# A sliding-window attention and FFN block: attention moved from token-major to channel-major layout

## Chip, cores and metric

The kernel runs on one core of a Trainium2 chip. The metric is the device time of one execution in microseconds (us). A core has five engines that each work through their own instructions in order and wait for each other by semaphores: TensorE (PE; its weight loads are listed apart as PEld), VectorE (DVE), ScalarE (ACT), GpSimd (POOL) and SyncE (SP, which issues most transfers).

## What is computed

With x of 2048 tokens by 640 channels, 32 heads of 20 channels, a window of 8 tokens with dilation 2, and an FFN of width 1536, all in bf16 at the interface:

```python
xn = layernorm(x)
q, k, v = split(xn @ wqkv)                       # 32 heads of 20 channels each
idx = pos[:, None] - 2 * arange(8)[None, :]      # the 8 tokens that a token attends to
logits = einsum("bhsd,bhswd->bhsw", q, k[idx]) * 20 ** -0.5
logits = where(idx >= 0, logits, -1e9)
o = einsum("bhsw,bhswd->bhsd", softmax(logits), v[idx])
out = x + o @ wo + (gelu_tanh(xn @ w1 + b1) @ w2 + b2)
```

## The kernel before

The 2048 tokens are taken in four blocks `n` of 512 tokens (`CH`), each of four pieces `bl` of 128 tokens. Channels are five tiles of 128 (`KT`). All weights are loaded at the start, nearly all by SP, in the order in which the code issues them: four pieces of x, the rest of x (`x_all`), the Q and K weights (`wqk_sb`), V's weights, `b1_rt`, `b2bc`, the two FFN weights, and the output projection `wo2`.

- Layer norm (`ln_units`): DVE takes statistics of all tokens at the start, ACT normalizes one piece, PE transposes it, and ACT copies it to `xnT` (channels on partitions, tokens free).
- Q and K (`qk_units`, L241, L252) come out with channels on partitions, as `qTn` and `kTn`. `kTn` has 14 columns ahead, taken from the block before, so a shift by 2w tokens is a slice.
- V (`v_units`, L267, L270) comes out with tokens on partitions. ACT copies it and writes it to DRAM (`v_tok`). `issue_vwin` (L298) reads it back through POOL's queue, as `vwin`, eight shifted copies of each piece, 1280 KB each.
- Logits (`logit_units`): for a half block of 256 tokens (`pr`) and a window position `w`, DVE multiplies Q by the shifted K (`prod`, L380). Then PE takes each 128x128 part of `prod` as weights and multiplies it by `ind`, 128x32, which sums the channels of each head (L388). The result `lg` has tokens on partitions and (window position, head) in the free dimension.
- Softmax (`softmax_unit`, L342 to L364): maximum, subtraction, `exp` on ACT, sum, reciprocal, `attn`, by half block.
- Weighted sum of V (`av_units`): DVE multiplies `vwin` by `attn` (L415) and adds the upper four window positions to the lower (L421); PE adds the remaining four by matmuls against `ident` and transposes in doing so (L439); ACT copies to `oTn`.
- FFN (`ffn1_units`, L314, L321) and output (`out_units`, L465 to L494): an output piece is one PSUM sum of 12 FFN tiles, 5 attention tiles and x + b2 (`xb2`), in a pair of tiles `ops_lo` (512 columns) and `ops_hi` (128). ACT copies it out.

The order of work is written out by hand: `interleave` puts one or two `fillers` (FFN, next block's layer norm, Q, K, V) ahead of each `prod` step, and `inserts` say after which step the softmax and the weighted sum stand. Four PSUM banks (`psum1`) serve all but the logits and the output.

Of the kernel before, what the change touches and what calls it, by code (L numbers as in the profile page):

```python
# [12 lines left out]
ALU = mybir.AluOpType  # L14
# [6 lines left out]
def kernel(  # L21
# [11 lines left out]
):  # L33
    nc = tc.nc
# [15 lines left out]
    HP = 2 * P  # L50
    NPR = BPC // 2
    WH = W // 2
    SCALE = float(DH) ** -0.5
    EPS = 1e-5
    A3 = 0.044715
    GC = math.sqrt(2.0 / math.pi)
    SQA3 = math.sqrt(A3)
    PADC = PAD + CH
    PSW = 2 * CH

    assert Bb == 1 and D == KT * P and F == FT * P and S == NCH * CH
    assert P == 4 * H and FT % 2 == 0 and BPC % 2 == 0 and NCH == 4
# [7 lines left out]
    dram = ctx.enter_context(tc.tile_pool(name="dram", bufs=1, space=bass.MemoryType.DRAM))  # L70
    psum1 = ctx.enter_context(tc.tile_pool(name="psum1", bufs=4, space=bass.MemoryType.PSUM))
    psumL = ctx.enter_context(tc.tile_pool(name="psumL", bufs=2, space=bass.MemoryType.PSUM))
    psumO = ctx.enter_context(tc.tile_pool(name="psumO", bufs=2, space=bass.MemoryType.PSUM))

    ident = consts.tile([P, P], BF16, name="ident")
    make_identity(nc, ident[:])

    x0p = ctx.enter_context(tc.tile_pool(name="x0p", bufs=1))
    x0 = x0p.tile([P, BPC, D], BF16, name="x0")
    for bl in range(BPC):  # L80
        nc.sync.dma_start(x0[:, bl, :], x_nb[:, bl, :])
    tmp = tc.alloc_tile_pool(name="tmp", bufs=1, side="right")
    x_all = tmp.tile([P, NB, D], BF16, name="x_all")
    for c in range(1, NCH):
        nc.sync.dma_start(x_all[:, c * BPC : (c + 1) * BPC, :], x_nb[:, c * BPC : (c + 1) * BPC, :])
    wqk_sb = wts.tile([P, KT, 2 * D], BF16, name="wqk_sb")
    wqkv_v = A_wqkv.rearrange("(t p) n -> p t n", p=P)
    nc.sync.dma_start(wqk_sb[:, :, 0:D], wqkv_v[:, :, 0:D])
    nc.sync.dma_start(wqk_sb[:, :, D : 2 * D], wqkv_v[:, :, D : 2 * D])
    wv_raw = tmp.tile([P, KT, D], BF16, name="wv_raw")  # L90
    nc.sync.dma_start(wv_raw[:], wqkv_v[:, :, 2 * D : 3 * D])
    b1_rt = tmp.tile([P, P], BF16, name="b1_rt")
    nc.sync.dma_start(b1_rt[0:FT, :], B_b1.rearrange("(t p) -> t p", p=P))
    b2bc = consts.tile([P, D], BF16, name="b2bc")
    b2_bcast = bass.AP(tensor=B_b2.tensor, offset=B_b2.offset, ap=[[0, P], [1, D]])
    nc.sync.dma_start(b2bc[:], b2_bcast)
    w1_sb = wts.tile([P, KT, F], BF16, name="w1_sb")
    nc.sync.dma_start(w1_sb[:], B_w1.rearrange("(t p) n -> p t n", p=P))
# [3 lines left out]
    for t in range(KT):  # L102
        for q in range(4):
            src = bass.AP(
                tensor=A_wo.tensor,
                offset=A_wo.offset + (4 * t + q) * D,
                ap=[[DH * D, H], [1, D]],
            )
            nc.sync.dma_start(wo2[q * H : (q + 1) * H, t, :], src)
    zeros = tmp.tile([P, D], BF16, name="zeros")  # L110
    nc.vector.memset(zeros[:], 0.0)
    v_tok = dram.tile([PAD + S, D], BF16, name="v_tok")
    nc.sync.dma_start(v_tok[0:PAD, :], zeros[0:PAD, :])

    ind_f = tmp.tile([P, KT, H], F32, name="ind_f")
    nc.gpsimd.memset(ind_f[:], 1.0)
    nc.gpsimd.affine_select(
        out=ind_f[:],
        in_=ind_f[:],
        pattern=[[P, KT], [-DH, H]],  # L120
        compare_op=ALU.is_ge,
        fill=0.0,
        base=0,
        channel_multiplier=1,
    )
    nc.gpsimd.affine_select(
        out=ind_f[:],
        in_=ind_f[:],
        pattern=[[-P, KT], [DH, H]],
        compare_op=ALU.is_ge,  # L130
        fill=0.0,
        base=DH - 1,
        channel_multiplier=-1,
    )
    ind = consts.tile([P, KT, H], BF16, name="ind")
    nc.vector.tensor_copy(ind[:], ind_f[:])
    eps_t = consts.tile([P, 1], F32, name="eps_t")
# [5 lines left out]
    mv_all = tmp.tile([P, NB, nc.vector.BN_AGGR_DIM], F32, name="mv_all")
    std_all = tmp.tile([P, NB], F32, name="std_all")
    rstd_all = consts.tile([P, NB], F32, name="rstd_all")
    negmb_all = consts.tile([P, NB], F32, name="negmb_all")
    for sl, src, boff in ((slice(0, BPC), x0, 0), (slice(BPC, NB), x_all, BPC)):
        for b in range(sl.start, sl.stop):
            stats = tmp.tile([P, 2, nc.vector.BN_STATS_DIM], F32, name=f"stats{b}")
            xb_ = src[:, b, :] if src is x_all else src[:, b, :]  # L150
            nc.vector.bn_stats(stats[:, 0, :], xb_[:, 0 : D // 2])
            nc.vector.bn_stats(stats[:, 1, :], xb_[:, D // 2 : D])
            nc.vector.bn_aggr(mv_all[:, b, :], stats[:])
        nc.scalar.activation(std_all[:, sl], mv_all[:, sl, 1], ACT.Sqrt, bias=eps_t[:], scale=1.0)
        nc.vector.reciprocal(rstd_all[:, sl], std_all[:, sl])
        nc.vector.scalar_tensor_tensor(
            out=negmb_all[:, sl],
            in0=mv_all[:, sl, 0],
            scalar=-1.0,
            in1=rstd_all[:, sl],  # L160
            op0=ALU.mult,
            op1=ALU.mult,
        )
    b1_tp = psum1.tile([P, PSW], BF16, tag="acc1", name="b1_tp")
# [3 lines left out]
    for ti in range(KT):  # L168
        nc.vector.tensor_copy(
            out=wv_perm[:, ti, :].rearrange("p (d h) -> p d h", d=DH),  # L170
            in_=wv_raw[:, ti, :].rearrange("p (h d) -> p d h", d=DH),
        )

    tmp.release()

    xtp = ctx.enter_context(tc.tile_pool(name="xtp", bufs=2))
    ktp = ctx.enter_context(tc.tile_pool(name="ktp", bufs=2))
    qtp = ctx.enter_context(tc.tile_pool(name="qtp", bufs=2))
    lnp = ctx.enter_context(tc.tile_pool(name="lnp", bufs=3))
    vsp = ctx.enter_context(tc.tile_pool(name="vsp", bufs=2))  # L180
    prodp = ctx.enter_context(tc.tile_pool(name="prodp", bufs=2))
    smp = ctx.enter_context(tc.tile_pool(name="smp", bufs=2))
    atp = ctx.enter_context(tc.tile_pool(name="atp", bufs=6))
    vwp = ctx.enter_context(tc.tile_pool(name="vwp", bufs=3))
    avp = ctx.enter_context(tc.tile_pool(name="avp", bufs=1))
    otp = ctx.enter_context(tc.tile_pool(name="otp", bufs=1))
# [486 lines left out]
```

## Time and profile before

| | before |
|---|---|
| time, median of 3 runs | 288.19 us (286.31 to 289.06) |
| profiled execution: time | 287.44 us |
| profiled execution: span, first to last instruction | 285.3 us |
| mean granted TensorE clock | 0.976 of full speed |
| busy: PE, DVE, ACT, POOL | 242.8, 169.4, 136.1, 17.9 us |
| HBM read, written | 35.56 MB, 5.26 MB |

The profile is one execution. Busy time of PE includes the tail of each matmul, in which the next one runs already. In its rows, `line engine op out<-in xcount | busy us, mean ns | idle before it <- who ended that idle time`; in a row of the timeline, the first two numbers are the start and the length in us.

### The profile page before, as it was taken

Reading aid. Unit: us, or ns where it says so; the run is one execution under the profiler, and the core shown is the slowest. Engines: PE = TensorE matmul, PEld = TensorE weight load, DVE = VectorE, ACT = ScalarE, POOL = GpSimd, SP = SyncE. Lnnn points to the kernel's source line nnn. Section 1 sums busy time; section 2 is a strip of 40 time slices with the busy share of each in tenths; the row PEclk is TensorE's granted clock in tenths of the full one; section 3 lists DMA queues with packets and bytes.
Section 4 is the critical chain, followed back from the end, with each engine's and each line's share of the span. In section 5 each row is a group of like instructions: output and inputs, shape, how many; then the busy total and the mean of one; then the engine's idle time right before and its main releaser. Section 6 shows DMA issues by size and latency. Waiting matters only on the chain. (4 is left out here: it accounts for less than half of the span.)

```text
span 285.3 us, 5189 instructions
## 1 busy us (share of the span) xinstructions
PE 242.8 (85%) x2177; PEld 140.7 (49%) x2217; DVE 169.4 (59%) x221; ACT 136.1 (48%) x240; POOL 17.9 (6%) x29
## 2 busy tenths in 40 slices
PE   0028996539999999999899999999899999998895
PEld 0023453414455645566565445566555565565552
DVE  5892041817436517449994614799997876618810
ACT  1333559149647977452227884532226753332221
POOL 2000022000100000001111000001101111100000
PEclk9999999559999999999999999999999999999999
DMA  6999339940602010024767000026666287551010
GB/s 200 368 381 355 83 115 317 361 146 4 229 3 75 32 36 0 2 92 160 245 231 258 32 0 3 23 71 233 207 232 210 60 294 239 166 176 38 30 37 25
DMA packets 20507, 41.15 MB, mean 144 GB/s; under 512 B 1782, under 2 KB 15748, under 8 KB 20484
## 3 DMA queue, kind: packets, MB, share of 16 engines
q0 software_dynamic: 4352, 20.97, 21.1%
q1 hardware_dynamic: 11524, 14.61, 16.2%
q10 hardware_dynamic: 4608, 5.24, 5.2%
q8 instruction: 17, 0.28, 0.4%
q14 instruction: 6, 0.05, 0.0%
HBM read 35.56 MB, written 5.26 MB: 143 GB/s over the span
## 5 line engine op out<-in xcount | busy, mean ns | idle before, releaser
L380 DVE TENSOR_TENSOR prod<-qTn,kTn 128x1280 bf16<-128x1280 bf16 x64 | 51.0, 820 | 60.3 <-PE lg L388 43.6
L314 PE MATMUL hps<-xnT,w_sb 128*128 128x512 bf16 x233 | 55.4, 384 | 0.9 <-ACT hTn L321 0.3
L481 PE MATMUL ops_lo<-w_sb,hTn 128*128 128x512 bf16 x177 | 52.2, 380 | 3.2 <-ACT osb L492 3.1
L415 DVE TENSOR_TENSOR avprod<-vwin,attn 128x5120 bf16<-128x5120 bf16 x16 | 45.1, 2820 | 8.4 <-PE oacc_hi L439 8.4
L241 PE MATMUL qkps<-xnT,wqk_sb 128*128 128x512 bf16 x194 | 47.4, 391 | 1.3 <-ACT xnT L212 1.0
L484 PE MATMUL ops_hi<-w_sb,hTn 128*128 128x128 bf16 x192 | 42.2, 220 | 0.8 <-issue 0.2
L314 PEld LDWEIGHTS <-w_sb 128*128 128x128 bf16 x240 | 23.1, 99 | 26.6 <-issue 2.2
L321 ACT ACTIVATE hTn<-hps,b1T 128x512 bf16<-128x512 f32 x48 | 31.2, 688 | 6.5 <-PE hps L314 5.9
L388 PEld LDWEIGHTS <-prod 128*128 128x128 bf16 x640 | 23.0, 97 | 16.3 <-DVE prod L380 9.3
L388 PE MATMUL lg<-ind,prod 128*128 128x32 bf16 x640 | 25.7, 178 | 5.6 <-DVE prod L380 5.4
L241 PEld LDWEIGHTS <-wqk_sb 128*128 128x128 bf16 x200 | 18.9, 100 | 22.6 <-issue 3.9
L481 PEld LDWEIGHTS <-hTn 128*128 128x128 bf16 x192 | 18.7, 98 | 19.5
L492 ACT CAST osb<-ops_lo 128x512 bf16<-128x512 f32 x16 | 9.4, 585 | 39.6 <-PE ops_lo L481 39.5
L446 ACT CAST oT<-oacc_lo 128x512 bf16<-128x512 f32 x16 | 9.3, 584 | 31.4 <-PE oacc_lo L439 31.0
L421 DVE TENSOR_TENSOR avprod<-avprod 128x2560 bf16<-128x2560 bf16 x16 | 23.6, 1475 | 0.2
L298 POOL DMA_DIRECT2D vwin<-v_tok x16 | 14.3, 891 | 144.7 <-DVE avprod L415 139.8
L481 PE MATMUL ops_lo<-wo,oT 128*128 128x512 bf16 x74 | 22.3, 379 | 0.1
L267 PE MATMUL vlo<-wv_perm,xnT 128*128 128x512 bf16 x75 | 22.0, 379 | 0.0
L439 PEld LDWEIGHTS <-avprod 128*128 128x128 bf16 x320 | 18.1, 98 | 6.2 <-DVE avprod L421 5.7
L484 PEld LDWEIGHTS <-hTn 128*128 128x128 bf16 x192 | 18.7, 98 | 4.3 <-issue 4.1
L439 PE MATMUL oacc_lo<-ident,avprod 128*128 128x128 bf16 x256 | 17.0, 219 | 2.2 <-DVE avprod L421 2.0
L484 PE MATMUL ops_hi<-wo,oT 128*128 128x128 bf16 x80 | 17.5, 219 | 0.3
(59 smaller groups left out, 240.1 us busy)
## 6 DMA issues: line engine op xcount, KB each, us to landing
vwin<-v_tok POOLq DMA_DIRECT2D x16, 1280.0 KB, 7.1
w_sb<-in_B_w_dram SPq DMA_DIRECT2D x2, 1920.0 KB, 17.5
v_tok<-v_sb ACTq DMA_DIRECT2D x16, 160.0 KB, 1.8
xb<-in_A_x_dram SPq DMA_DIRECT2D x16, 160.0 KB, 5.3
out_dram<-osb ACTq DMA_DIRECT2D x16, 160.0 KB, 2.4
x_all<-in_A_x_dram SPq DMA_DIRECT2D x3, 640.0 KB, 7.5
xt<-in_A_x_dram SPq DMA_DIRECT2D x12, 160.0 KB, 2.8
wqk_sb<-in_A_wqkv_dram SPq DMA_DIRECT2D x2, 800.0 KB, 10.4
```

Source lines behind the costliest of these rows:

```text
L241: nc.tensor.matmul(ps[:], lhsT=wqk_sb[:, ti, to * P : (to + 1) * P], rhs=xnT[:, ti, :], start=(ti == 0), stop=(ti == KT - 1),)
L267: nc.tensor.matmul(vlo[:], lhsT=lhs, rhs=wv_perm[:, ti, 0:CH], start=(ti == 0), stop=(ti == KT - 1))
L298: nc.gpsimd.dma_start(vwin[:], vsrc)
L314: nc.tensor.matmul(hps[:], lhsT=w1_sb[:, ti, ft * P : (ft + 1) * P], rhs=xnT[:, ti, :], start=(ti == 0), stop=(ti == KT - 1),)
L321: nc.scalar.activation(hTn[:, ft, :], hps[:], ACT.Gelu_apprx_tanh, bias=b1T[:, ft : ft + 1], scale=1.0)
L380: nc.vector.tensor_tensor(out=prod[:], in0=qTn[:, :, pr * HP : (pr + 1) * HP], in1=kTn[:, :, PAD - DIL * w + pr * HP : PAD - DIL * w + (pr ...
L388: nc.tensor.matmul(lg[:, q * HP + w * H : q * HP + (w + 1) * H], lhsT=prod[:, t, q * P : (q + 1) * P], rhs=ind[:, t, :], start=(t == 0), s ...
L415: nc.vector.tensor_tensor(out=avprod[:].rearrange("p w (d h) -> p w d h", d=DH), in0=vwin[:].rearrange("p w (d h) -> p w d h", d=DH), in1= ...
L421: nc.vector.tensor_tensor(out=avprod[:, 0:WH, :], in0=avprod[:, 0:WH, :], in1=avprod[:, WH:W, :], op=ALU.add,)
L439: nc.tensor.matmul(dst, lhsT=avprod[:, j, t * P : (t + 1) * P], rhs=ident[:], start=(j == 0), stop=(j == WH - 1),)
L481: nc.tensor.matmul(ops_lo[:], lhsT=lhs, rhs=rhs[:, 0:CH], start=(k == 0), stop=(k == nk - 1))
L484: nc.tensor.matmul(ops_hi[:, 0 : D - CH], lhsT=lhs, rhs=rhs[:, CH:D], start=(k == 0), stop=(k == nk - 1),)
```

## The change

Attention stays on chip in one layout, channels on partitions and tokens free.

- V is projected like Q and K, to `vT` with 14 columns ahead; `v_tok`, `vwin` and their transfers go. `wqkv_sb` is loaded as a whole, by ACT's queue. Q, K and V take their weights with a stride of five columns (L189), so that partition p holds channels of head p // 4.
- Logits: DVE forms `prod` for two window positions and the whole block. PE takes the constant `head_of` (128x32) as weights and streams `prod`, 256 columns at a time (two window positions of one 128-token piece j). The output of piece j goes to partitions 32j to 32j+31, so that four matmuls in a row use four column tiles of the array. `L` has (piece, head) on partitions and (window position, token in the piece) in the free dimension; the mask is a matmul of `ones_r` by `maskrow`.
- Softmax is done once per block on all 128 partitions. PE subtracts the maximum in PSUM (`negident`), and sums the exponentials over the window (`ident`). `attn` is spread from heads to channels by matmuls with 32 rows of `rep` and copied by ACT to `ax`.
- The weighted sum is on DVE alone (`pv`, L284 to L297), by slices of `vT`.
- Layer norm's statistics are taken block by block, and DVE, not ACT, normalizes. Units are written in plain order (last lines below), and the tile framework's scheduler sets the order on each engine. The logits' PSUM (`psL`) is two banks, `lo` and `hi` of the output have one each (`psO`), and four banks (`psA`) serve the rest.

```diff
-            nc.gpsimd.dma_start(vwin[:], vsrc)
...
-                        nc.tensor.matmul(
-                            lg[:, q * HP + w * H : q * HP + (w + 1) * H],
-                            lhsT=prod[:, t, q * P : (q + 1) * P],
-                            rhs=ind[:, t, :],
...
-                        nc.tensor.matmul(
-                            dst,
-                            lhsT=avprod[:, j, t * P : (t + 1) * P],
-                            rhs=ident[:],
...
+        wv = wqkv_sb[:, :, which * D : (which + 1) * D].rearrange("p t (c r) -> p t r c", r=KT)
+        for to in range(KT):
+            ps = psA.tile([P, CH], F32, tag="acc", name="pps")
+            for ti in range(KT):
+                nc.tensor.matmul(
+                    ps[:],
+                    lhsT=wv[:, ti, to, :],
+                    rhs=xnT[:, ti, :],
+                    start=(ti == 0),
+                    stop=(ti == KT - 1),
+                )
+            nc.scalar.copy(body[:, to, :], ps[:])
...
+    def logits(n):
+        qT, kT = qTs[n], kTs[n]
+        L = psL.tile([P, W, P], F32, tag="L", name="L")
+        for wp in range(W // 2):
+            prod = prodp.tile([P, 2, KT, CH], BF16, tag="prod", name="prod")
+            for i in range(2):
+                off = PAD - DIL * (2 * wp + i)
+                nc.vector.tensor_tensor(
+                    out=prod[:, i, :, :], in0=qT[:], in1=kT[:, :, off : off + CH], op=ALU.mult
+                )
+            for t in range(KT):
+                for j in range(BPC):
+                    nc.tensor.matmul(
+                        L[j * H : (j + 1) * H, 2 * wp : 2 * wp + 2, :],
+                        lhsT=head_of[:],
+                        rhs=prod[:, :, t, j * P : (j + 1) * P],
+                        start=(t == 0 and wp % 2 == 0),
+                        stop=False,
+                        skip_group_check=True,
+                    )
+        if n == 0:
+            for g in range(2):
+                nc.tensor.matmul(
+                    L[0:H, 4 * g : 4 * g + 4, :],
+                    lhsT=ones_r[:],
+                    rhs=maskrow[:, 4 * g : 4 * g + 4, :],
+                    start=False,
+                    stop=False,
+                    skip_group_check=True,
+                )
+        return L
+    def softmax(n, L):
+        m = smp.tile([P, P], BF16, tag="m", name="m")
+        nc.vector.tensor_reduce(out=m[:], in_=L[:].rearrange("p w c -> p c w"), axis=AX.X, op=ALU.max)
+        for g in range(2):
+            nc.tensor.matmul(
+                L[:, 4 * g : 4 * g + 4, :],
+                lhsT=negident[:],
+                rhs=m[:].unsqueeze(1).to_broadcast([P, 4, P]),
+                start=False,
+                stop=True,
+                skip_group_check=True,
+            )
+        e = smp.tile([P, W, P], BF16, tag="e", name="e")
+        nc.scalar.activation(e[:], L[:], ACT.Exp, scale=SCALE)
+        ssum = psA.tile([P, P], F32, tag="acc", name="ssum")
+        for w in range(W):
+            nc.tensor.matmul(ssum[:], lhsT=ident[:], rhs=e[:, w, :], start=(w == 0), stop=(w == W - 1))
+        rs = smp.tile([P, P], F32, tag="rs", name="rs")
+        nc.vector.reciprocal(rs[:], ssum[:])
+        attn = smp.tile([P, W, P], BF16, tag="attn", name="attn")
+        nc.vector.tensor_tensor(
+            out=attn[:], in0=e[:], in1=rs[:].unsqueeze(1).to_broadcast([P, W, P]), op=ALU.mult
+        )
+        ax = axp.tile([P, W, CH], BF16, tag="ax", name="ax")
+        for g in range(2):
+            for j in range(BPC):
+                xps = psA.tile([P, CH], F32, tag="acc", name="xps")
+                nc.tensor.matmul(
+                    xps[:],
+                    lhsT=rep[j * H : (j + 1) * H, :],
+                    rhs=attn[j * H : (j + 1) * H, 4 * g : 4 * g + 4, :],
+                    start=True,
+                    stop=True,
+                )
+                nc.scalar.copy(
+                    ax[:, 4 * g : 4 * g + 4, j * P : (j + 1) * P], xps[:].rearrange("p (w c) -> p w c", w=4)
+                )
+        return ax
+    def av(n, ax):
+        vT = vTs[n]
+        tiles = []
+        for wp in range(W // 2):
+            pv = prodp.tile([P, 2, KT, CH], BF16, tag="prod", name="pv")
+            for i in range(2):
+                w = 2 * wp + i
+                off = PAD - DIL * w
+                nc.vector.tensor_tensor(
+                    out=pv[:, i, :, :],
+                    in0=vT[:, :, off : off + CH],
+                    in1=ax[:, w, :].unsqueeze(1).to_broadcast([P, KT, CH]),
+                    op=ALU.mult,
+                )
+            tiles.append(pv)
+            if wp % 2 == 1:
+                a = tiles[wp - 1]
+                nc.vector.tensor_tensor(out=a[:], in0=a[:], in1=pv[:], op=ALU.add)
+        a, b = tiles[0], tiles[2]
+        nc.vector.tensor_tensor(out=a[:], in0=a[:], in1=b[:], op=ALU.add)
+        oT = otp.tile([P, KT, CH], BF16, tag="oT", name="oT")
+        nc.vector.tensor_tensor(out=oT[:], in0=a[:, 0, :, :], in1=a[:, 1, :, :], op=ALU.add)
+        oTs[n] = oT
...
+    def attention(n):
+        L = logits(n)
+        ax = softmax(n, L)
+        av(n, ax)
+
+    ln(0)
+    qkv(0)
+    ln(1)
+    for n in range(NCH):
+        attention(n)
+        ffn1(n)
+        if n + 1 < NCH:
+            qkv(n + 1)
+        if n + 2 < NCH:
+            load_x(n + 2)
+            ln(n + 2)
+        if n > 0:
+            outs(n - 1)
+    outs(NCH - 1)
```

Layer norm (`ln`, L142 to L171), `ffn1` and `outs` do the same sums as before, except for the points above; in `outs` (L325 to L343) the `ident` term with `xb2` stands ahead of the five attention tiles.

What stands on PE where logits meet other work, before (block 1's logits, an output pair of block 0, a transpose):

```order
L388 LDWEIGHTS prod
L388 MATMUL lg<-ind,prod 128x32
L481 LDWEIGHTS hTn
L481 MATMUL ops_lo<-w_sb,hTn 128x512
L484 LDWEIGHTS hTn
L484 MATMUL ops_hi<-w_sb,hTn 128x128
L209 LDWEIGHTS xn
L209 MATMUL tp<-ident,xn 128x128
```

And after, on PE in block 1, where the second pair of window positions ends and output matmuls of block 0 follow:

```order
L215 LDWEIGHTS head_of
L215 MATMUL L<-prod,head_of 32x256
L336 LDWEIGHTS hT
L336 MATMUL lo<-w_sb,hT 128x512
L337 LDWEIGHTS hT
L337 MATMUL hi<-w_sb,hT 128x128
```

The weights of a logit matmul are now a constant and `prod` streams; the groups hold 20 matmuls of 256 columns instead of 10 of 32. Further down in the same block, on PE, the softmax's sum stands between output matmuls:

```order
L336 LDWEIGHTS oT
L336 MATMUL lo<-wo_122,oT 128x512
L337 LDWEIGHTS oT
L337 MATMUL hi<-wo_122,oT 128x128
L252 LDWEIGHTS ident
L252 MATMUL ssum<-e,ident 128x128
```

In block 1, 17 output matmuls follow the sum before the `xps` matmuls begin, and 8 more stand between those; in block 0 nothing stands there, since no output is ready.

On DVE at the start, before (V's weights are reordered, then the first `prod` of block 0):

```order
L169 COPY wv_perm<-wv_raw 128x640
L167 CAST b1T<-b_tp 128x12
L169 COPY wv_perm<-wv_raw 128x640 x3
L380 TENSOR_TENSOR prod<-qTn,kTn 128x1280 x5
L465 TENSOR_TENSOR xb_1041<-xb,b2bc 128x640
```

And after, on DVE at the same place (`xc` in these rows is block 2's x; the two `xn` are block 1's):

```order
L147 BN_STATS stats<-xc 128x6
L149 BN_AGGR mv<-stats 128x2
L148 BN_STATS stats<-xc 128x6
L327 TENSOR_TENSOR xb_1208<-xb,b2bc 128x640
L210 TENSOR_TENSOR prod<-qT,kvT 128x2560 x4
L157 TENSOR_SCALAR xn<-xc,mv,rstd 128x640 x2
```

The first `prod` of block 0 now stands behind the statistics of block 2 and an `xb`, so behind their transfers. A little later on DVE, between the maximum and the reciprocal of block 0 (`xc` is block 3's x):

```order
L148 BN_STATS stats<-xc 128x6
L327 TENSOR_TENSOR xb_1254<-xb,b2bc 128x640
L149 BN_AGGR mv<-stats 128x2
L254 RECIPROCAL rs<-ssum 128x128
L256 TENSOR_TENSOR attn<-e,rs 128x1024
```

These are the last of six statistics, three aggregations and an `xb` that stand behind the maximum `m` and ahead of the reciprocal; the blocks after have one `xb` there.

More of the change, by code (lines that the diff above doesn't have):

```diff
@@ L2 @@
-import math
 from contextlib import ExitStack
@@ L78 @@
[L78 to L86, printed above, removed]
@@ L143 @@
[L143 to L163, printed above, removed]
```

605 lines of the change are left out of this document (137 added, 468 removed).

## Prediction

> **What bounds the kernel now.** I read the busy table first, then busy time by stage, then the groups of instructions, and last single instructions in order of time.
>
> ```profile
> PE 242.8 (85%) x2177; PEld 140.7 (49%) x2217; DVE 169.4 (59%) x221; ACT 136.1 (48%) x240; POOL 17.9 (6%) x29
> ```
>
> ```profile
> 0.00:23.00 23.00, 2.72 (x22) 2.34 (x23) 18.43 (x62) 7.70 (x11) 1.64 (x10) 1.00 0.94 321
> 23.00:38.00 15.00, 14.95 (x66) 6.61 (x66) 1.57 (x3) 6.61 (x12) 0.90 (x1) 1.00 0.58 176
> 48.00:60.00 12.00, 3.72 (x64) 3.18 (x65) 7.23 (x11) 3.12 (x5) 0.00 (x0) 0.62 0.95 336
> 60.00:73.00 13.00, 11.07 (x64) 5.49 (x67) 6.74 (x13) 11.55 (x16) 0.31 (x1) 0.83 0.14 41
> 262.00:286.00 24.00, 17.71 (x147) 10.57 (x148) 8.91 (x6) 4.71 (x14) 0.00 (x0) 1.00 0.08 28
> ```
>
> The second fence is five stages: length, then busy time of PE, PEld, DVE, ACT, POOL, then granted clock, DMA share, GB/s. TensorE sets the end. It is idle 20.3 of the first 23 us, 8.3 us from 48 to 60 (transfers fill that stage at 0.95, and the granted clock falls to 0.62), 1.9 from 60 to 73, and 6.3 in the last stage; everywhere else it is nearly full. So a change counts by what it does to TensorE's work and to those holes.
>
> Since matmuls overlap, TensorE's work must come from paces, not from mean durations.
>
> ```profile
> 25.20 0.58 ACT L252 CAST qTn<-qkps 128x512 bf16<-128x512 f32 x1 [2.38 <-PE qkps L241]
> 27.25 0.58 ACT L252 CAST qTn<-qkps 128x512 bf16<-128x512 f32 x1 [1.47 <-PE qkps L241]
> 28.33 0.58 ACT L252 CAST qTn<-qkps 128x512 bf16<-128x512 f32 x1 [0.49 <-PE qkps L241]
> 35.88 0.58 ACT L252 CAST kTn<-qkps 128x512 bf16<-128x512 f32 x1 [0.49 <-PE qkps L241]
> 276.76 0.38 PE L481 MATMUL ops_lo<-w_sb,hTn 128*128 128x512 bf16 x1 [0.62 <-ACT osb L492]
> 281.38 0.38 PE L481 MATMUL ops_lo<-xb,ident 128*128 128x512 bf16 x1
> 281.59 0.22 PE L484 MATMUL ops_hi<-xb,ident 128*128 128x128 bf16 x1
> 272.35 1.07 PE L439 MATMUL oacc_lo<-ident,avprod 128*128 128x128 bf16 x16
> 46.18 0.65 PE L388 MATMUL lg<-ind,prod 128*128 128x32 bf16 x20
> ```
>
> - From 28.33 to 35.88 seven groups of five pass: 7.55/35 = 0.216 us for 512 columns. The first two groups took twice that after the idle start, which cost about 2.1 us.
> - From 276.76 to 281.38 stand 17 pairs of the output (512 and 128 columns): 0.272 a pair. Between output blocks that follow each other the first row shows 0.62 idle, about 0.78 of pace lost, since the PSUM pair is copied out first.
> - Sixteen 128-column matmuls in 1.07, the last counted 0.22: 0.057 each. Twenty 32-column ones in 0.65, the last 0.18: 0.025 each.
>
> Before, TensorE's work is thus 440 x 0.216 (Q, K, first FFN layer) + 368 pairs x 0.272 (V, output) + 640 x 0.025 (logits) + 400 x 0.057 (transposes, sum of V) = 95.0 + 100.1 + 16.0 + 22.8 = 233.9. The remaining 51 us of the 285.3 span are the start, the hole with its slow clock, small waits, and the end.
>
> **The change: TensorE's work.** After: 540 x 0.216 (Q, K, V, first layer) = 116.6; 288 output pairs = 78.3; 80 transposes and 32 sums of exponentials x 0.057 = 6.4; 42 matmuls of 512 columns (negated maximum, attention spread over channels, mask) x 0.216 = 9.1; and 320 logit matmuls of 256 columns into four column tiles. The 320 `oacc` matmuls (18.2) go.
>
> The logit price is the open one. One at a time, half of 512 columns is 0.108; four at a time it is 0.027, next to the 0.025 of the short logits of before, which shows that instructions can be issued so fast. I take 0.04 (12.8 in all): the four tiles are independent and their outputs lie on different partitions, so it is nearest to the 0.025 row; the surplus is for starting one behind the other. Ends kept: 0.025 and 0.108.
>
> The Trainium skill, "TensorE: Matmul & The Clock Gate", Part 3, gives 2.38x for three column tiles of 512 columns. Estimated from that page, 0.108/2.38 = 0.045 would add 1 us to the sum; no run here shows it yet.
>
> Sum: 223.2, 10.7 under before.
>
> **The start.**
>
> ```profile
> 0.81 1.80 SPq L81 DMA_DIRECT2D x<-in_A_x_dram  x4
> 3.09 0.49 DVE L151 BATCH_NORM_STATS2 stats<-x 128x6 f32<-128x320 bf16 x1 [1.77 <-DMA x<-in_A_x_dram]
> 18.66 0.10 PEld L165 LDWEIGHTS <-b_rt 12*128 12x128 bf16 x1 [18.66 <-DMA b_rt<-in_B_b_dram]
> x_all<-in_A_x_dram SPq DMA_DIRECT2D x3, 640.0 KB, 7.5
> wqk_sb<-in_A_wqkv_dram SPq DMA_DIRECT2D x2, 800.0 KB, 10.4
> wv_raw<-in_A_wqkv_dram SPq DMA_DIRECT2D x1, 800.0 KB, 12.1
> GB/s 200 368 381 355 83 115 317 361 146 4 229 3 75 32 36 0 2 92 160 245 231 258 32 0 3 23 71 233 207 232 210 60 294 239 166 176 38 30 37 25
> ```
>
> Before, PE's first row waits 18.66 us for `b_rt`, queued on SP behind 5 MB (x, `x_all`, `wqk_sb`, `wv_raw`); the first projection starts at 22.9. After, `b1_rt` stands behind 0.66 MB and the QKV weights go out on ACT's queue. What bounds then: 3.8 MB (x of two blocks, QKV weights) at some 370 GB/s is 10 us after 3 us of delay, with a share for `w1`; and DVE takes the second block's statistics before `rstd`. I take 16 us to the first projection (bounds 13, and 22.9 as before), so 14.9 idle plus 1.1 of transposes, and 2.1 for the slow first groups. It ends at 16 + 16.2 + 2.1 = 34.3.
>
> **Block 0, which nothing covers.** DVE's order puts statistics of block 2 and `xb_1208` ahead of the first `prod`. Counted by their shapes, 9.35 MB end with these (three blocks of x, 2.0; QKV, 2.5; both FFN weights, 3.9; `wo2` and `b2bc`, 1.0); the GB/s row (slices of 7.1 us) moved 9.3 MB by 28.5, and `xb_1206` is issued once the first piece of block 2 has landed: about 30.5. So `prod` starts at 31, though K is ready near 29.5.
>
> ```profile
> L380 DVE TENSOR_TENSOR prod<-qTn,kTn 128x1280 bf16<-128x1280 bf16 x64 | 51.0, 820 | 60.3 <-PE lg L388 43.6 <-ACT kTn L252 16.7
> L421 DVE TENSOR_TENSOR avprod<-avprod 128x2560 bf16<-128x2560 bf16 x16 | 23.6, 1475 | 0.2
> L415 DVE TENSOR_TENSOR avprod<-vwin,attn 128x5120 bf16<-128x5120 bf16 x16 | 45.1, 2820 | 8.4 <-PE oacc_hi L439 8.4
> L342 DVE TENSOR_REDUCE mx<-lg 128x64 f32<-128x512 f32 x8 | 5.5, 688 | 4.6 <-PE lg L388 4.6
> L364 DVE TENSOR_TENSOR attn<-e,rs 128x512 bf16<-128x512 f32 x8 | 5.5, 684 | 0.1
> L362 DVE RECIPROCAL rs<-ssum 128x64 f32<-128x64 f32 x8 | 4.4, 547 | 0.1
> L151 DVE BATCH_NORM_STATS2 stats<-x_all 128x6 f32<-128x320 bf16 x12 | 5.7, 476 | 1.2 <-DMA x_all<-in_A_x_dram 1.2
> L465 DVE TENSOR_TENSOR xb<-xb,b2bc 128x640 bf16<-128x640 bf16 x16 | 7.8, 486 | 12.6 <-PE ops_hi L484 7.4 <-DMA xb<-in_A_x_dram 5.2
> L352 ACT ACTIVATE e<-e 128x512 f32<-128x512 f32 x8 | 5.0, 630 | 8.5 <-DVE e L346 8.4
> 37.19 0.58 ACT L278 CAST v_sb<-vlo 128x512 bf16<-128x512 f32 x1 [0.72 <-PE vlo L267]
> 37.67 0.27 ACT L279 CAST v_sb<-vhi 128x128 bf16<-128x128 f32 x1
> ```
>
> A `prod` of 2560 costs 1.475 by L421: eight take 11.8, with two `xn` 12.5, done at 43.5; last logits and mask 44.6. No row has the softmax's new sizes; I double the rows of half the size and take off one fixed part of 0.165, which L380 and L421 give (2 x 820 - 1475). Maximum over 1024: 2 x 0.688 - 0.165 = 1.21. Negation 0.5 (two matmuls and a tail). `exp`: 1.1 by L352. But between maximum and reciprocal DVE has six half-block statistics and an `xb` (4.0 us by L151, L465), longer than PE and ACT need there, so the reciprocal starts at 49.9; 128 elements by L362 cost 0.93, `attn` 1.20 by L364: 52.2 with waits. (The ends are the undoubled row and twice it, 0.2 to 0.5 us to a step.) Eight `xps` are copied by ACT, 0.48 apart as in the last two rows, and the first layer gets its PSUM at 55.1. From 34.3 to 55.1 TensorE has 7.4 us of work: a **hole of 13.4**, and 2.2 for a slow clock after it, as at 25.20. That is also what a block costs where no other work covers its softmax.
>
> **Blocks 1 to 3.** Here the output matmuls of the block before fill the softmax. Block 1's `prod` starts when K is copied (81.7) and ends at 94.2, PE's projections end at 86.5; 61 output matmuls in between leave 2.5 idle, and the first layer of block 1 starts at 104.2. In blocks 2 and 3 DVE's `prod` ends some 8 us before PE asks for the last pair; the waits left are PSUM copies and the `attn` chain, 2.5 and 3.0 us, 1.0 of each for changing between tile shapes. DVE per block: 11.8 `prod`, 3.4 softmax, 21.7 for `pv` and its sums (8 x 1.475 + 3 x 2.82 + 1.475), 7 for layer norm and `xb`: 44 of a cycle of 56, so it binds in blocks 0 and 1 alone.
>
> **The end.** Block 3's output follows block 2's: six boundaries x 0.78 = 4.7. After the last matmul before needs 285.3 - 281.8 = 3.5; unchanged.
>
> **Transfers.**
>
> ```profile
> vwin<-v_tok POOLq DMA_DIRECT2D x16, 1280.0 KB, 7.1
> POOL vwin L298 <- DVE avprod L415: 139.8, 13, 39.9
> ```
>
> The V windows go (20.97 MB) with V's way through DRAM. They filled the stage from 48 to 60; their other waits are POOL's alone, so I count only that stage, which is in the 51 us above. After has no such transfers.
>
> **Sum.** 223.2 + 14.9 + 2.1 + 13.4 + 2.2 + 2.5 + 2.5 + 3.0 + 4.7 + 3.5 = 272.0 us of span. The profiled execution took 287.44 at a span of 285.3, 2.1 more: 274.1. The median of the runs shown is 288.19, 0.75 above it.
>
> **Rivals.**
>
> 1. *Column tiles take turns* (0.108 each). Added per logit matmul: 0.068; 20 show in block 0 (1.4), 80 in each of blocks 2 and 3 (5.5 each), and 5.0 in block 1, where part fell into DVE's time: 17.4, span 289.4, time 291.5, **slower** by 1.4%. It turns from faster to slower at 0.04 + 0.068 x 13.3/17.4 = 0.092. For it: no row of before has two tiles at once. Against: nothing orders one tile behind another.
>
> 2. *Weight loads stop the tiles too.*
>
> ```profile
> L314 PEld LDWEIGHTS <-w_sb 128*128 128x128 bf16 x240 | 23.1, 99 | 26.6 <-issue 2.2
> ```
>
> If each logit matmul also waits for its own load of 0.099, it costs 0.207: 43 us more, 317. The row speaks against: 240 loads of 99 ns are hidden beside matmuls that come every 0.216. The Trainium skill, same page, "What overlaps and what doesn't", says that loads overlap matmuls in flight only where the row groups differ; column tiles share their rows, so by that rule this rival holds. For full-width matmuls of one row group this trace disagrees (0.216 and 99 ns); for column tiles no row shows it.
>
> 3. *Strided weights.* L193 loads every fifth column of the QKV weights; before they lie side by side. Up to 0.216 a load is hidden: nothing. At three times 99 ns, 300 x 0.08 = 24 us more, 298. Against: the margin is twofold.
>
> 4. *Tile shape drains.* If every change between shapes costs a matmul's full tail (0.38 - 0.216 = 0.16), 16 changes a block cost 2.6, not 1.0: 279. The Trainium skill, "TensorEngine Tiling (Array Packing)", "Key Properties", says that a change of tiling mode drains TensorE; the 0.16 is my reading of this trace, no run shows it for tiles.
>
> 5. *Late transfers.* Each us that the pieces before block 0's `prod` come later than 31 is one us at the end; 5 later gives 279.
>
> **How the numbers follow.** Forecast with 4 and 5, all well under 284.6: 0.66. A logit price between, or several small losses together: 0.04 faster still, 0.10 within 1%. Rival 1: 0.13 slower. Rivals 2 and 3: 0.07 slower (0.03 and 0.04). One per cent, 2.9 us, is what a measurement can tell: faster 0.70, same 0.10, slower 0.20. The low end takes 0.025 per logit matmul (3.8 less), tile changes at nothing (2) and a start 4 us earlier that the transfers allow through: 264. The high end is rival 1: 292; what lies beyond is 2 and 3.
>
> **What would show it.** Right: logit groups of 20 in under 1.1 us; PE idle about 13 us between 34 and 55 with the granted clock down; `m`, reciprocal and `attn` in later blocks beside output matmuls; first projection near 16 us. Wrong: 20 logit matmuls in 2.2 us or more; `prod` or `pv` above 1.5 us each; L193 at a pace above 0.216; in blocks 2 and 3 PE waiting for `prod`.

## The result

The changed kernel takes 275.57 us (median of 4 runs, 274.68 to 276.86) where the kernel before takes 287.25 on the same chip (4 runs, 286.15 to 289.06): ratio 0.959, 95% interval 0.952 to 0.967, **4% faster**. The prediction had 274.1. The profiled execution took 276.86 at a span of 275.1, the longest of the four; before it was 287.44 at 285.3.

The busy table of the profile after:

```profile
PE 233.7 (85%) x1564; PEld 122.4 (44%) x1591; DVE 173.0 (63%) x191; ACT 125.0 (45%) x212; POOL 0.9 (0%) x8
HBM read 12.62 MB, written 2.62 MB: 55 GB/s over the span
```

TensorE has 9.1 us less of busy time, DVE 3.6 more. TensorE's share is the same 85%: it still sets the end, with holes of about the same size as before, only elsewhere. Busy time by stage, columns as in the prediction:

```profile
0.00:20.70 20.70, 3.27 (x22) 2.10 (x23) 11.49 (x47) 4.42 (x7) 0.88 (x8) 1.00 0.93 320
39.10:59.20 20.10, 10.53 (x121) 4.94 (x119) 16.32 (x29) 10.01 (x17) 0.00 (x0) 0.68 0.14 41
59.20:90.30 31.10, 30.77 (x133) 15.15 (x136) 25.21 (x16) 19.37 (x31) 0.00 (x0) 0.94 0.01 1
90.30:108.90 18.60, 15.98 (x177) 8.89 (x179) 13.12 (x14) 9.39 (x17) 0.00 (x0) 1.00 0.06 19
138.00:167.50 29.50, 27.49 (x257) 15.31 (x260) 16.39 (x17) 14.19 (x26) 0.00 (x0) 1.00 0.15 46
```

The hole of before (48 to 73, transfers at 0.95) is gone. In its place stands block 0's own: from 39.1 to 59.2 TensorE works 10.5 of 20.1 us, with transfers at 0.14 and the granted clock at 0.68. What TensorE does there and ahead of it, in order of time:

```profile
18.37 0.59 PE L193 MATMUL pps<-xnT,wqkv_sb 128*128 128x512 bf16 x1 [0.84 <-ACT xnT L168]
20.70 18.59 PE L193 MATMUL pps<-xnT,wqkv_sb 128*128 128x512 bf16 x73 [1.74 <-DMA wqkv_sb<-in_A_wqkv_dram]
43.82 0.73 PE L215 MATMUL L<-prod,head_of 128*32 128x256 bf16 x20 [1.36 <-DVE prod L210]
50.15 1.01 PE L240 MATMUL L<-m,negident 128*128 128x512 bf16 x2 [1.32 <-DVE m L238]
52.55 1.01 PE L252 MATMUL ssum<-e,ident 128*128 128x128 bf16 x8 [1.39 <-ACT e L249]
55.95 0.61 PE L263 MATMUL xps<-attn,rep 32*128 32x512 bf16 x4 [2.38 <-DVE attn L256]
57.22 2.05 PE L263 MATMUL xps<-attn,rep 32*128 32x512 bf16 x4 [0.67 <-ACT ax L270]
59.20 0.61 PE L307 MATMUL hps<-xnT,w_sb 128*128 128x512 bf16 x1
74.13 16.35 PE L193 MATMUL pps<-xnT,wqkv_sb 128*128 128x512 bf16 x74
```

From 43.82 to 57.22 each row waits for a result of the chain from `prod` through the softmax to `ax`, and the first FFN layer (L307), which needs none of it, stands behind. Twenty logit matmuls take 0.73 us.

### The profile page after: what moved, and what is told of

Its sections match the earlier page's. It is cut to its first block, busy times and chain, and to the rows that moved or that the text cites. A ratio compares the mean times of both kernels' runs of the same rounds, so it can differ in the third digit from the quotient of the medians.

```text
span 275.1 us, 3746 instructions
## 1 busy us (share of the span) xinstructions
PE 233.7 (85%) x1564; PEld 122.4 (44%) x1591; DVE 173.0 (63%) x191; ACT 125.0 (45%) x212; POOL 0.9 (0%) x8
## 4 chain that ended last, share of the span: by engine, by line
PE 71%; DVE 12%; ACT 7%; DMA 7%; issue 2%; SPq 0%; DVEq 0%; ACTq 0%
PE lo L336 20%; PE hps L307 19%; PE pps L193 18%; DVE prod L210 10%; PE hi L337 6%; DMA wqkv_sb<-in_A_wqkv_dram 4%; ACT osb L341 3%; PE xps L263 3%; DMA xc<-in_A_x_dram 3%; PE L L215 2%; ACT ax L270 1%; PE ssum L252 1%; ACT L249 1%; DVE m L238 1%; ACT e L249 1%
## 5 line engine op out<-in xcount | busy, mean ns | idle before, releaser
L193 PE MATMUL pps<-xnT,wqkv_sb 128*128 128x512 bf16 x296 | 68.0, 390 | 2.8 <-DMA wqkv_sb<-in_A_wqkv_dram 1.7
L336 PE MATMUL lo<-w_sb,hT 128*128 128x512 bf16 x177 | 52.4, 379 | 5.2 <-ACT osb L341 4.9
L210 DVE TENSOR_TENSOR prod<-qT,kvT 128x2560 bf16<-128x2560 bf16 x32 | 45.5, 1484 | 17.6 <-ACT kvT L200 17.6
L307 PE MATMUL hps<-xnT,w_sb 128*128 128x512 bf16 x235 | 54.0, 388 | 0.4 <-issue 0.2
L284 DVE TENSOR_TENSOR pv<-kvT,ax 128x2560 bf16<-128x2560 bf16 x32 | 45.5, 1484 | 10.4 <-ACT ax L270 10.4
L193 PEld LDWEIGHTS <-wqkv_sb 128*128 128x128 bf16 x300 | 35.6, 119 | 34.7 <-DMA wqkv_sb<-in_A_wqkv_dram 3.3
L337 PE MATMUL hi<-w_sb,hT 128*128 128x128 bf16 x192 | 42.2, 220 | 0.6
L314 ACT ACTIVATE hT<-hps,b1T 128x512 bf16<-128x512 f32 x48 | 32.6, 687 | 15.8 <-PE hps L307 15.4
L307 PEld LDWEIGHTS <-w_sb 128*128 128x128 bf16 x240 | 23.9, 100 | 30.1 <-issue 3.6
L200 ACT CAST kvT<-pps 128x512 bf16<-128x512 f32 x40 | 23.4, 585 | 18.9 <-PE pps L193 18.9
L336 PEld LDWEIGHTS <-hT 128*128 128x128 bf16 x192 | 18.7, 98 | 24.2 <-issue 4.0
L336 PE MATMUL lo<-wo,oT 128*128 128x512 bf16 x77 | 23.1, 379 | 0.0
L337 PEld LDWEIGHTS <-hT 128*128 128x128 bf16 x192 | 18.7, 97 | 9.5 <-issue 8.8
L200 ACT CAST qT<-pps 128x512 bf16<-128x512 f32 x20 | 11.7, 585 | 15.0 <-PE pps L193 15.0
L215 PE MATMUL L<-prod,head_of 128*32 128x256 bf16 x320 | 12.2, 283 | 3.7 <-DVE prod L210 3.6
## 6 DMA issues: line engine op xcount, KB each, us to landing
w_sb<-in_B_w_dram SPq DMA_DIRECT2D x2, 1920.0 KB, 12.2
```

The costliest lines, as they stand in the source:

```text
L193: nc.tensor.matmul(ps[:], lhsT=wv[:, ti, to, :], rhs=xnT[:, ti, :], start=(ti == 0), stop=(ti == KT - 1),)
L200: nc.scalar.copy(body[:, to, :], ps[:])
L210: nc.vector.tensor_tensor(out=prod[:, i, :, :], in0=qT[:], in1=kT[:, :, off : off + CH], op=ALU.mult)
L215: nc.tensor.matmul(L[j * H : (j + 1) * H, 2 * wp : 2 * wp + 2, :], lhsT=head_of[:], rhs=prod[:, :, t, j * P : (j + 1) * P], start=(t == 0 ...
L284: nc.vector.tensor_tensor(out=pv[:, i, :, :], in0=vT[:, :, off : off + CH], in1=ax[:, w, :].unsqueeze(1).to_broadcast([P, KT, CH]), op=ALU ...
L307: nc.tensor.matmul(hps[:], lhsT=w1_sb[:, ti, ft * P : (ft + 1) * P], rhs=xnT[:, ti, :], start=(ti == 0), stop=(ti == KT - 1),)
```

## The experiments

All were timed in three rounds beside the kernel before on the same chip; ratios are to it.

**1. The loop order of the logit matmuls turned.** In the code as it stands the token blocks (column tiles) change fastest.

```diff
-            for t in range(KT):
-                for j in range(BPC):
+            for j in range(BPC):
+                for t in range(KT):
```

> The changed kernel with the two inner loops of the logits swapped, so that five matmuls in a row go to the same column tile; same matmuls, same work. Theory (four column tiles stream at the same time, and that is why 320 matmuls cost so little): 20 of them take about 2.2 us instead of the 0.73 of the changed kernel's rows, 0.108 each. At 0.084 more for each that shows (20 in block 0, some 50 in block 1, 80 in blocks 2 and 3), 19 us more: about 295 us, slower than before. Rival (the logits lie beside DVE's prod or other waits, so their price hardly counts): under 280 us. Rival (it is not the tiles but short issue: pace set by issue alone): 20 still take 0.7 us, no change.

Measured: 277.26 us (275.52 to 281.0), ratio 0.958 (0.950 to 0.965), as the changed kernel and far from the 295 expected. Twenty matmuls took 1.09 instead of 0.73:

```profile
41.11 1.09 PE L215 MATMUL L<-prod,head_of 128*32 128x256 bf16 x20 [0.89 <-DVE prod L210]
```

So the expectation that tiles would run one after the other was wrong: 20 strictly in turn are 20 x 0.108 = 2.2. The length fits a queue for each tile: 15 issues at 0.025 until the last tile's first, then its five at 0.107, then a tail of 0.17, 1.08 in all. That reading is argued from the length alone. Nor is the order free because the times agree: in this profile the first FFN layer began at 55.88 instead of 59.20 (the weights, for one, were there at 19.30 instead of 20.70), and the last matmul came at the same 271.46, so 3.3 us were lost in between. The experiment did not take the column tiles away, and another was needed.

**2. The logits without column tiles.** Every logit matmul fills all 128 output partitions, with zeros in the weights outside its own 32 columns; the loops stand as in experiment 1.

```diff
-                        L[j * H : (j + 1) * H, 2 * wp : 2 * wp + 2, :],
-                        lhsT=head_of[:],
+                        L[:, 2 * wp : 2 * wp + 2, :],
+                        lhsT=wide[:, (3 - j) * H : (3 - j) * H + P],
```

> The changed kernel with the logits made on the whole array: a weight tile of 128 columns that holds the head map in the 32 columns of token block j and zeros elsewhere, so that every logit matmul fills all 128 output partitions and the four token blocks add into one another. Same sums, same order of t within a block, no column tiles. Theory (the four column tiles work at once; 20 matmuls take 0.73 us): without them 20 matmuls of 256 columns take 20 x 0.107 = 2.1 to 2.2 us, 1.4 to 1.6 more for each of 16 pairs of window steps. In blocks 1 to 3, where TensorE is the bound, 12 x 1.5 = 18; in block 0 VectorE's products (2.97 a pair) cover three of four pairs, so 1.5 there. Time 275.6 + 19 to 20 = 294 to 296. Rival (the tiles' overlap is worth nothing in time, since VectorE's products set the pace of the logits in every block): 277 to 280, with waits of TensorE for prod shrinking by as much as the matmuls grow.

Measured: 300.03 us (297.2 to 301.14), ratio 1.038 (1.031 to 1.046): **slower than the kernel before**, and above the 294 to 296 of the theory. The groups by line, of this kernel and then of the changed kernel:

```profile
L218 PE MATMUL L<-prod,wide 128*128 128x256 bf16 x320 | 36.6, 273 | 0.0
```

```profile
L215 PE MATMUL L<-prod,head_of 128*32 128x256 bf16 x320 | 12.2, 283 | 3.7 <-DVE prod L210 3.6
```

```profile
40.95 8.46 PE L218 MATMUL L<-prod,wide 128*128 128x256 bf16 x76
```

The same 320 matmuls take 36.6 us instead of 12.2; a run of 76 goes at 0.111 each. Of the 24.4 more, the 3.6 of waiting for `prod` are paid anyway: 20.8, and the spans differ by 295.4 - 275.1 = 20.3. I had put 1.4 to 1.6 on a pair of window steps and left out three of block 0's four pairs; it was 1.5 on all of them, less those waits. The two profiles are of the shortest execution here and the longest of the changed kernel; by the ratios the difference is about 23, and what makes up the rest is open. Without four tiles at once the change loses.

**3. The kernel before with little traffic.** Of each V window only one of eight positions is brought, the others are zeros, so the attention sum is left incomplete.

```diff
-                ap=[[D, P], [-DIL * D, W], [1, D]],
+                ap=[[D, P], [-DIL * D, 1], [1, D]],
...
-            nc.gpsimd.dma_start(vwin[:], vsrc)
+            nc.gpsimd.dma_start(vwin[:, 0:1, :], vsrc)
```

> The kernel before, but each V window transfer brings one of eight window positions (160 instead of 1280 KB); the other seven stay zeros written once at the start, so the attention sum is left incomplete; all instructions of the engines remain. Theory (the hole of TensorE from 48 to 60 us and its slow clock to 73 are made by these transfers, which delay x and xb): the hole goes, 8.3 + 1.9 us idle and some 2 us of slow clock, about 275 us, as fast as the changed kernel. Rival (the hole comes from the order, prod waiting for PSUM of the logits): 284 to 288 us.

Measured: 279.49 us (277.59 to 280.02), ratio 0.966 (0.961 to 0.971), between the 275 of the theory and the 284 to 288 of the rival. The two stages of the hole of before:

```profile
48.00:60.00 12.00, 9.45 (x118) 5.77 (x119) 8.69 (x20) 10.63 (x14) 0.54 (x1) 1.00 0.42 119
60.00:73.00 13.00, 13.00 (x82) 6.15 (x81) 3.29 (x5) 9.39 (x16) 0.00 (x0) 1.00 0.10 26
```

TensorE was idle 8.3 + 1.9 us there and now 2.6, and the clock stays at 1.00. The windows cost the kernel before 8.8 us (288.31 on that chip), most of it in this one hole. Rows of the kernel before show how:

```profile
47.75 0.49 DVE L465 TENSOR_TENSOR xb<-xb,b2bc 128x640 bf16<-128x640 bf16 x1 [2.70 <-DMA xb<-in_A_x_dram]
50.72 0.49 DVE L465 TENSOR_TENSOR xb<-xb,b2bc 128x640 bf16<-128x640 bf16 x1 [2.48 <-DMA xb<-in_A_x_dram]
52.00 0.45 PE L388 MATMUL lg<-ind,prod 128*128 128x32 bf16 x10 [4.13 <-DVE prod L380]
60.69 1.73 ACT L204 ACTIVATE xn<-xt,negmb_all,rstd_all 128x640 bf16<-128x640 bf16 x2 [4.74 <-DMA xt<-in_A_x_dram]
61.66 0.61 PE L209 MATMUL tp<-ident,xn 128*128 128x128 bf16 x4 [5.01 <-ACT xn L204]
```

TensorE waited for a `prod` that stood on DVE behind two `xb`, and for an `xn` that ACT makes from `xt`. Both are rows of x, 160 KB a transfer, and they came late. No engine waited for a window itself. The windows filled the queues, and the x rows took up to 8.3 us (`xb`) and 8.9 us (`xt`) to land; in this experiment it was at most 4.4 and 4.1.

Together with experiment 2 this says where the gain went. Some 9 us come from the transfers and, by the prediction's paces, 10.7 from TensorE's work; only 11.7 arrived. That block 0's new hole took the missing 8 is a sum of parts, not measured by itself; experiment 9 gets about 8.5 back by filling that hole.

**4. The changed kernel with as much traffic that nobody waits for.** After V of a block is made, POOL copies 8 x 128 rows of x to an unused buffer in HBM, four times a block, as the windows were read before.

```diff
+                nc.gpsimd.dma_start(dumps[b][0:1, 0, 0:CH], dest[0:1, KT - 1, PAD : PAD + CH])
+                nc.gpsimd.dma_start(dumps[b][:], dsrc)
```

> The changed kernel with 21 MB more of HBM reads (and as many writes), which nobody waits for: for each token block 8 x 128 rows of x are copied from HBM to an unused HBM buffer, issued on GpSimd when V of the block is made, at the place where the kernel before brought its V windows. Theory (the windows cost the kernel before time because TensorE and VectorE waited for them, not because they filled the queues): 275 to 278. Rival (the traffic itself delays the loads of x, of residual rows and the stores that the kernel needs): 280 to 288, with waits that name a DMA in blocks 0 to 2.

Measured: 276.1 us (273.78 to 277.12), ratio 0.956 (0.950 to 0.962): no cost. Its block 0, and two of its transfers beside those of the changed kernel:

```profile
39.00:59.00 20.00, 10.44 (x109) 4.57 (x105) 16.22 (x30) 10.14 (x18) 5.77 (x8) 0.63 0.90 295
xb<-in_A_x_dram SPq DMA_DIRECT2D x16, 160.0 KB, 7.9
out_dram<-osb ACTq DMA_DIRECT2D x16, 160.0 KB, 5.6
```

```profile
xb<-in_A_x_dram SPq DMA_DIRECT2D x16, 160.0 KB, 2.2
out_dram<-osb ACTq DMA_DIRECT2D x16, 160.0 KB, 1.8
```

The queues are nearly as full as before (0.90 to 0.95), residual rows take 7.9 us instead of 2.2, stores 5.6 instead of 1.8, and TensorE works the same 10.4 us of 20. Here the delay costs nothing, since no engine needs those rows when they are late. For the kernel before the theory is not right: no engine waited for the windows, and it was by filling the queues that they made x rows late, which DVE and ACT needed at once (experiment 3).

**5. Q, K and V weights in three tiles.**

```diff
-    wqkv_sb = wts.tile([P, KT, 3 * D], BF16, name="wqkv_sb")
+    wqkv_s = [wts.tile([P, KT, D], BF16, name=f"wqkv_sb{s}") for s in range(3)]
```

> The changed kernel with Q, K and V weights in three tiles, so the first projection waits for Q's transfer alone. Theory (the 4.7 us that the first projection came later than forecast are its second weight load, which waits for all three transfers; block 0 passes every us on to the end): projections start when xnT is there, 18.4 instead of 20.7, and the end comes 2.3 us earlier, about 273.3 us. Rival (prod of block 0 waits for block 2's transfers anyway, as I forecast): no change within 0.5 us.

Measured: 274.59 us (272.52 to 275.65), ratio 0.950 (0.944 to 0.955). The projections run through from 17.86:

```profile
17.86 17.90 PE L193 MATMUL pps<-xnT,wqkv_sb 128*128 128x512 bf16 x75 [0.84 <-ACT xnT L168]
```

In the changed kernel the first weight load ran at 17.22, and the second waited until 20.70, when the last of the three transfers into the one tile landed (issued at 9.3, 11.4 us on its way), though it reads Q's weights alone. With three tiles no load waits. The first projections end at 17.86 + 17.90 = 35.8 instead of 20.70 + 18.59 = 39.3, 3.5 us earlier. Between the medians 1.0 us of it shows, between the ratios 2.7, and the intervals overlap, so the size stays uncertain. The wait itself varies: in other runs with one tile it ends between 19.2 (experiment 9) and 21.1 (experiment 2).

**6. The first FFN layer of block 0 ahead of its attention.**

```diff
+        if n == 0:
+            ffn1(n)
         attention(n)
-        ffn1(n)
+        if n > 0:
+            ffn1(n)
```

> The changed kernel with block 0's first FFN layer written ahead of block 0's attention. Theory (block 0's hole of some 12.7 us is there because no work stands in the order that could fill it, not because of a resource): TensorE runs 13 us of FFN while DVE forms prod, and output matmuls fill the softmax: 9 to 11 us faster, about 266 us. Rival (the work is only moved: outputs of block 0 are then missing as filler in block 1, and ACT's GELUs delay the softmax): 272 to 276 us.

Measured: 274.08 us (269.27 to 275.15). The runs lie too far apart for an interval. This decides nothing between the theory's 266 and the rival's 272 to 276.

**7. The same with the FFN layer between logits and softmax,** `ln(2)` behind it, the weights in three tiles, and every second `lo` and `hi` of the last `outs` in the banks of `psA`.

> The changed kernel with Q, K and V weights in three tiles, ffn1(0) and ln(2) placed between logits(0) and softmax(0), and every second lo and hi of the last outs in the other PSUM pool. Theory (block 0's waits are order, not work): the separate weights give 1.0 to 2.5 as they did before, the three last output boundaries lose 0.6 each (1.8), block 0's hole of some 9 us is filled by the first FFN layer of block 0, and what is left open is that VectorE then starts the weighted sum of V of block 0 at 62 and has 22 us of it, so that the logits of block 1 wait for their products for 4 to 7 us after qkv(1). Time 266 to 270. Rival (the hole only moves to block 1 in full): 272 to 274.

Measured: 271.22 us (270.39 to 272.24), ratio 0.940 (0.935 to 0.946). Between the 266 to 270 of the theory and the 272 to 274 of the rival. Its block 0 and block 1 by stage, and its longest wait there:

```profile
40.00:60.00 20.00, 19.64 (x145) 9.66 (x144) 11.68 (x26) 18.39 (x25) 0.00 (x0) 1.00 0.12 35
80.00:100.00 20.00, 13.49 (x127) 6.90 (x126) 18.89 (x13) 4.18 (x9) 0.00 (x0) 0.83 0.03 9
PE lo L340 <- DVE oT L297: 4.8, 1, 4.8
```

The hole in block 0 is filled (19.6 of 20), and a new one of 6.5 us opens in block 1, where DVE is busy 18.9 of 20 with the weighted sum and the next products and TensorE waits for `oT`.

**8. The first FFN layer of blocks 0 and 1 ahead,** the rest as in 7 but for `ln(2)`, which stays where it was.

```diff
+        L = logits(n)
+        if n == 0:
+            ffn1(n)
+        ax = softmax(n, L)
+        av(n, ax)
+        if n > 1:
+            ffn1(n)
         if n + 1 < NCH:
             qkv(n + 1)
+        if n == 0:
+            ffn1(1)
```

> The changed kernel with Q, K and V weights in three tiles, ffn1(0) between logits(0) and softmax(0), ffn1(1) right after qkv(1), and every second lo and hi of the last outs in the other PSUM pool. Theory: as the kernel with ffn1(0) alone moved, and ffn1(1) (13.1 us) stands beside VectorE's weighted sum of V of block 0, so that the logits of block 1 find most of their products made: TensorE idle before its first projection 14.5, in the softmax of blocks 0 and 1 about 5 each, of blocks 2 and 3 about 2.5 each, output boundaries 3, end 3.5, on 233 of work: span 265 to 268, time 266 to 270, and 2 to 4 below the kernel with ffn1(0) and ln(2) moved. Rival (VectorE is late again in block 1 since its own work there, 22 of weighted sum and 12 of products, is longer than the 29.5 that TensorE has): no better than that kernel, 270 to 273.

Measured: **261.51 us** (261.16 to 262.21), ratio 0.907 (0.901 to 0.912), better than expected.

```profile
82.80 13.11 PE L307 MATMUL hps<-xnT,w_sb 128*128 128x512 bf16 x60
80.00:100.00 20.00, 20.00 (x175) 10.74 (x174) 18.02 (x14) 14.03 (x22) 0.00 (x0) 1.00 0.00 1
PE lo L340 <- ACT osb L345: 0.8, 2, 0.6
```

While DVE sums V of block 0 (18.0 of 20 busy), TensorE has block 1's first layer and is full. The waits for PSUM copies between output pieces, 4.9 in the changed kernel, are 0.8. I had credited three such boundaries; nearly all went.

**9. Of this, the order alone,** with the weights in one tile and the outputs' banks as in the changed kernel.

> Of the 261.5 us kernel only the order: ffn1(0) between logits(0) and softmax(0), ffn1(1) right after qkv(1); Q, K and V weights again in one tile and every lo and hi of the last outs again in its own bank. Theory (order is most of the gain over the changed kernel; the weights in three tiles are worth 1 to 2.8, the banks of the last outs 1.8 to 4): 265 to 268. Rival (the order alone does little, as it did with ffn1(0) alone at 274.1, and the two others carry the gain): 271 to 274.

Measured: 267.11 us (266.07 to 267.94), ratio 0.928 (0.921 to 0.935). So of 14 us under the changed kernel the order of two calls is worth about 8.5, the weights and the output banks about 5.6; these are differences of medians from different chips, and by the ratios they are 8.9 and 6.2.

## Why the prediction was right

The time was 1.5 us off, the span of the profiled execution 3.1 (275.1 for 272.0). Part of that closeness is luck, since errors cancel: block 0's projections ended 4.8 us late, its hole was 0.7 shorter, block 1 took 0.6 longer (49.7 for 49.1, from block 0's first FFN layer to its own), and from there to the last matmul it took 162.8 where the sum leaves 272.0 - 3.5 - 104.2 = 164.3. By its own steps:

- **TensorE's work and the logit price: right.** 320 x 0.04 = 12.8 was charged, 12.2 was busy. It is made of a tail for each group and 0.024 to 0.027 in the run: 20 in 0.73, and 51 in 1.60 in block 3:

```profile
208.85 1.60 PE L215 MATMUL L<-prod,head_of 128*32 128x256 bf16 x51
```

- The estimate of 0.045 from the Trainium skill's "TensorE: Matmul & The Clock Gate", Part 3, lies above the 12.2/320 = 0.038 measured with tails and well above 0.025 in the run; the page's figure is for three tiles of 512 columns.
- **Rival 1 (tiles in turn)** was priced at 17.4 us and slower than before; made real in experiment 2, it cost 20.3 of span and was slower. It was the right rival: what it asks decides the sign of the change.
- **Rival 2 (loads stop the tiles)** fails: 0.025 each leaves no room for a load in series, and 320 loads of 98 ns fill only 8.1 us, so they overlap each other too. The rule of the Trainium skill's "TensorE: Matmul & The Clock Gate", "What overlaps and what doesn't", does not hold in this trace, for column tiles either.

```profile
L215 PEld LDWEIGHTS <-head_of 128*32 128x32 bf16 x320 | 8.1, 98 | 6.9 <-issue 6.2
```

- **Rival 3 (strided weights)** fails: the strided loads take longer, 119 against 100 ns, and a block's 75 projections (74 of them recorded) still take 16.35, less the tail 0.216 each.

```profile
L193 PEld LDWEIGHTS <-wqkv_sb 128*128 128x128 bf16 x300 | 35.6, 119 | 34.7 <-DMA wqkv_sb<-in_A_wqkv_dram 3.3
L307 PEld LDWEIGHTS <-w_sb 128*128 128x128 bf16 x240 | 23.9, 100 | 30.1 <-issue 3.6
```

- **Rival 4 (shape drains)** is in part right: a change of shape has a price, less than the 0.16 of the rival. From a 512-column `xps` to the next matmul 0.32 us pass instead of 0.216, and from a 128-column `hi` to the first logit matmul 0.15 instead of 0.057, though the rows name no wait for another engine. That is about 0.1 a change, some 1.4 for the 14 changes of block 2, where 1.0 a block was charged and the rival had 2.6.

```profile
163.67 0.39 PE L263 MATMUL xps<-attn,rep 32*128 32x512 bf16 x1
163.99 0.23 PE L337 MATMUL hi<-w_sb,hT 128*128 128x128 bf16 x1
146.74 0.22 PE L337 MATMUL hi<-wo,oT 128*128 128x128 bf16 x1
146.89 0.61 PE L215 MATMUL L<-prod,head_of 128*32 128x256 bf16 x14
```

- **The start: 2.4 to 4.8 us too short.** The first projection came at 18.37, not 16, and the second matmul waited for the weights until 20.70. The prediction put 3.8 MB ahead of it, with "a share for `w1`"; by 20.70 some 320 GB/s x 20.7 us = 6.6 MB had moved, so that share was far larger. The projections of block 0 ended at 39.1, not 34.3. This term of the sum was mis-sized, and with it the span. Experiment 5 shows that the wait from 18.4 to 20.7 went with the weights in three tiles; the first projection itself starts at 17.9 there and in experiment 9, not at 16 either, since DVE made the first `xn` only at 14.0 (14.5 in the changed kernel).
- **Block 0's hole: right in length, wrong in what opens it.** From the end of the projections to the first FFN layer 20.8 were predicted and 20.1 measured. The first `prod` came at 34.55, not 31. ACT's copy of K released it, since the projections had waited for their weights; block 2's x and the `xb` (rival 5) were done on DVE 2.9 us earlier. With the weights in three tiles (second row, experiment 5) `prod` does start right behind that `xb`, at 31.13, and the first FFN layer at 55.13, as predicted.

```profile
34.55 5.70 DVE L210 TENSOR_TENSOR prod<-qT,kvT 128x2560 bf16<-128x2560 bf16 x4 [2.92 <-ACT kvT L200]
31.13 5.69 DVE L210 TENSOR_TENSOR prod<-qT,kvT 128x2560 bf16<-128x2560 bf16 x4
```

- **DVE's steps and the end: right.** `prod` 1484 ns (1475), maximum 1.22 (1.21), reciprocal 0.96 (0.93), `attn` 1.23 (1.20); after the last matmul 3.4 (3.5). One step of block 0 was wrong at little cost: the reciprocal waited 0.41 us for PE's `ssum` and not for DVE's statistics. The prediction also left out that ACT loads a table for 1.28 us ahead of `exp`.
- The transfers were counted as one stage inside "51 us of the rest". Experiment 3 puts their cost at 8.8 us, near the 8.3 + 1.9 idle that the prediction read there. But the prediction never asked whether the new hole is one of order; experiments 8 and 9 show that it is.

## What to carry to other kernels

Count the matmuls that use 32 of 128 output columns: four column tiles at once made 320 small matmuls three times cheaper and decided the sign of this change. A change that takes a wait away moves work forward to the next chain that nothing covers, so look for independent work, here a whole FFN layer, that can stand in that chain, and then for the engine that is late next (DVE in block 1). Full queues made the small transfers beside them late, and that costs where an engine needs one of these at once: it made a hole in the kernel before, and nothing in the changed kernel under as much traffic.

## What was not expected of the hardware

- Matmuls to the same column tile in a row do not stop those of other tiles: 20 in 1.09 us, not 2.2 (experiment 1).
- Four 32-row matmuls of 512 columns, on four row tiles, took 0.40 us together, hardly more than the 0.38 of one; 0.216 each had been charged:

```profile
161.29 0.40 PE L263 MATMUL xps<-attn,rep 32*128 32x512 bf16 x4
```

- The granted clock fell after gaps that are short. In the kernel of experiment 9, block 0's softmax left TensorE idle for no more than 1.29 and 0.65 us at a time; these are the gaps, and then its stages:

```profile
62.52 0.40 PE L263 MATMUL xps<-attn,rep 32*128 32x512 bf16 x4 [1.29 <-DVE attn L256]
63.56 2.05 PE L263 MATMUL xps<-attn,rep 32*128 32x512 bf16 x4 [0.65 <-ACT ax L270]
62.00:65.00 3.00, 1.58 (x7) 0.37 (x7) 0.86 (x2) 2.07 (x5) 0.00 (x0) 0.95 0.19 55
65.00:68.00 3.00, 2.97 (x7) 0.89 (x7) 2.99 (x3) 2.03 (x5) 0.00 (x0) 0.50 0.00 0
68.00:71.00 3.00, 2.95 (x14) 1.61 (x14) 3.00 (x3) 1.67 (x3) 0.00 (x0) 0.98 0.00 0
```

The clock was at 0.50 for about 3 us after them, in which 7 matmuls ran instead of 14. Whether the gaps or the 32-row matmuls between them brought it down was not tried.
